# Three buffers in place of two for the weight and activation parts on their way to DRAM, three in place of four for the raw weights on their way in, and theta's raw weights staged in the tiles of z

## The chip, the cores and the metric

The kernel runs on one core of one Trainium2 chip. The metric is device time in microseconds: the median over several runs of one launch, here 564.57 us over 3 runs (564.46 to 564.57). A profile is taken of one further execution of the same program; all durations below come from that execution.

## The reference

What is computed is an attention block followed by two mlp blocks, on 4 batches of 576 tokens with 512 channels (8 heads of 64):

```
scores = q k^T / 8, kept in a window of 32 (heads 0-3) or a window of 128 with every 4th key (heads 4-7)
x  = softmax(scores) v                        # attention, 4 batches
theta = x @ w_theta                           # first mlp ("moe")
zr, zi = x*cos(theta), x*sin(theta)
u  = x + w_tok_r zr + w_tok_i zi              # mixes tokens
x  = u + relu(u @ w_ch)
h  = relu(x @ w_in); u, v = halves of h       # second mlp ("moe2")
v  = layer_norm(v); v = w_spatial v + b_spatial
out = (u*v) @ w_out
```

Several weights (w_theta, w_tok_r, w_tok_i, w_ch, w_in, w_out) reach the kernel as 64-bit floats, and w_spatial as 32-bit floats.

## The kernel before, in words

Every large product is computed from parts: a number is split into a high part and the rest ("hi" and "lo", written as fp32r), and three matmuls (hi*hi, lo*hi, hi*lo) are summed in PSUM. So each weight and each activation passes through a short job before it is used. For a weight the job has these steps: a DMA brings a chunk of raw weights into a staging tile; for 64-bit weights `bits64` builds the 32-bit number with one scaling on ScalarE or GpSimd (L128 or L130) and three operations on VectorE (L131 to L133); one engine copies it into the high part (`copy`, L107 to L111) and one subtracts to get the low part (L144).

Three groups of staging tiles matter here, all rotating (a tile is written again when its last reader is done):

- `w64`: the raw 64-bit chunks, 128 x 576 words of 4 bytes, 2304 bytes in each partition. Four of them. They serve w_theta, w_tok, w_ch, w_in and w_out in turn. The last reader is the first of the three VectorE operations (L131), or the scaling, whichever is later.
- `stage`: the 32-bit number that `bits64` makes, and also the raw w_spatial chunks. Four of them.
- `parts`: a high and a low part side by side, 128 x 2 x 288 numbers, also 2304 bytes in each partition. Two of them. The second mlp's weights don't fit beside the first mlp, so they are split early and their parts are stored to DRAM (`stored`, L152 to L157), 32 times in all: 16 for w_in, 8 for w_spatial, 8 for w_out. The results of the first mlp for batches 0 to 2 go the same way (`ch_run`, L448 to L451), 24 times. A `parts` tile is free again when its store has landed.

The order of the program: attention of batch 0; theta and z of batch 0 (`th_unit`), while the first half of w_tok is prepared; then for each batch the token mixing (`tm_run`) with the attention of the next batch in between, the theta of the next batch, and the channel product (`ch_run`). Batches 2 and 3 are handled together: token mixing of batch 2 goes along with the attention of batch 3, and the 64 tokens left over of both share one theta unit (`th_shared`) that starts from a copy named `xs` (L332). After that follow token mixing and channel product of batch 3 and the second mlp, of dense matmuls. Which jobs of the second mlp's weights stand between which matmuls is set by rates in `spread` (L514, L520, L521).

Each engine runs its instructions in the order of the program. That order is fixed when the kernel is built: a scheduler places the instructions on each engine by its own estimate of durations, with the limits that the rotating tiles set. SyncE issues all DMAs, also in a fixed order, and an issue that must wait holds up those behind it. So a change in the number of buffers moves instructions on every engine, though no line of arithmetic is changed.

z is kept in `zh0` to `zh7` and `zl0` to `zl7`, 128 x 512 numbers each (`ztile`, L321); the first of them is written when the first theta unit with 128 tokens is through.

```
st = const.tile([P, 2 * CH], U32, tag="w64", name="w64", bufs=4)             # L120
t = const.tile([P, 2, CH], F32R, tag="parts", name="parts", bufs=2)[:, :, :n] # L155
pool, n_ = (const, 2) if b < B - 1 else (p2s, 8)                              # L448
h = pz.tile([P, DM], F32R, tag=f"zh{k}", name=f"zh{k}", bufs=bufs)            # L322
```

Of the kernel before, what the change touches and what calls it, by code (L numbers as in the profile page):

```python
# [11 lines left out]
F32 = mybir.dt.float32  # L12
F32R = mybir.dt.float32r
BF16 = mybir.dt.bfloat16
U32 = mybir.dt.uint32
# [6 lines left out]
B, H, S, D = 4, 8, 576, 64  # L22
DM = H * D
P = 128
HALF = S - 4 * P
CH = S // 2
# [5 lines left out]
NA = 6  # L32
NB = NT - NA
NEG = -4.0e9
MAGIC = 1.5 * 2.0**23
TURN = float(np.nextafter(np.float32(2 * math.pi), np.float32(0)))
INV2PI = float(np.float32(1.0 / (2.0 * math.pi)))
# [17 lines left out]
THETA_ENG = "gg"  # L55
# [7 lines left out]
def tile_block(ctx: ExitStack, tc: tile.TileContext, qT, kT, vw, eye_in, mask_in, eye_b_in, w_theta, w_tok, w_ch, w_in, w_sp, w_sph, b_sp, w_out, out):  # L63
# [3 lines left out]
    def f32(ap):  # L67
        return ap.bitcast(F32)


    const = ctx.enter_context(tc.tile_pool(name="const", bufs=1, side="left"))
# [1 line left out]
    dram = ctx.enter_context(tc.tile_pool(name="dram", bufs=1, space=DRAM))  # L73

    ident = const.tile([P, P], F32, name="ident")
    half_pi = const.tile([P, 1], F32, name="half_pi")
    magic = const.tile([P, 1], F32, name="magic")
    masks = const.tile([P, 4, 3, KW], BF16, name="masks")
    eye_b = const.tile([P, P], BF16, name="eye_b")
    V.memset(half_pi, math.pi / 2)  # L80
    V.memset(magic, MAGIC)

# [8 lines left out]
    pz = tc.alloc_tile_pool(name="pz", bufs=1, side="left")  # L91
# [4 lines left out]
    wth_h = pth.tile([P, 4, DM], F32R, name="wth_h")  # L96
    wth_l = pth.tile([P, 4, DM], F32R, name="wth_l")
# [14 lines left out]

    last_dma = [None]

    def bits64(src, n, eng):

        p = src.shape[0]
        st = const.tile([P, 2 * CH], U32, tag="w64", name="w64", bufs=4)  # L120
        last_dma[0] = SY.dma_start(st[:p, :2 * n], src.bitcast(U32))
        w = st[:p, :2 * n].rearrange("p (n w) -> p n w", w=2)
        lw, hw = w[:, :, 0], w[:, :, 1]
        g = const.tile([P, CH], F32, tag="stage", name="w64g", bufs=4)[:p, :n]
        c = c64[:p, :n].bitcast(U32)
        gi = g.bitcast(U32)
        if eng == "a":
            A.mul(g, hw.bitcast(F32), 2.0**-112)  # L128
        else:
            G.tensor_scalar(g, hw.bitcast(F32), 2.0**-56, 2.0**-56, op0=ALU.mult, op1=ALU.mult)  # L130
        V.tensor_scalar(c, lw, 29, None, op0=ALU.logical_shift_right)  # L131
        V.scalar_tensor_tensor(c, gi, 3, c, op0=ALU.logical_shift_left, op1=ALU.bitwise_or)
        V.scalar_tensor_tensor(gi, gi, 0x80000000, c, op0=ALU.bitwise_and, op1=ALU.bitwise_or)  # L133
        return g

    def split_weight(src, hi, lo, eng_hi, eng_lo, eng_bits="g"):
        n = hi.shape[-1]
        if src.dtype == F32:
            s = const.tile([P, CH], F32, tag="stage", name="stage", bufs=4)[:src.shape[0], :n]
            SY.dma_start(s, src)  # L140
        else:
            s = bits64(src, n, eng_bits)
        copy(hi, s, eng_hi)
        (G if eng_lo == "g" else V).tensor_tensor(lo, s, f32(hi), op=ALU.subtract)  # L144

# [6 lines left out]
    def stored(src, dst, k, cs, engs):  # L152

        n = cs.stop - cs.start
        t = const.tile([P, 2, CH], F32R, tag="parts", name="parts", bufs=2)[:, :, :n]  # L155
        split_weight(src[:, k, cs], t[:, 0], t[:, 1], *engs)
        SY.dma_start(f32(dst[:, k, :, cs]), f32(t))  # L157

    def w_theta_job(k, c):
        cs = slice(DM // 2 * c, DM // 2 * (c + 1))  # L160
        split_weight(w_theta[:, k, cs], wth_h[:, k, cs], wth_l[:, k, cs], *THETA_ENG)

    def w_tok_job(k, c):
        cs = slice(CH * c, CH * (c + 1))
# [268 lines left out]
    def ch_run(b):  # L433

        uh, ul = uu.pop(b)
        wch_h, wch_l = wch
        for c in range(2):
            cs = slice(CH * c, CH * (c + 1))
            for e in range(4):
                ps = ps_mm.tile([P, 512], F32, tag="mm", name="ps_r")  # L440
                n = 0
                for k in range(4):
                    for lh, rh in ((wch_h, uh), (wch_l, uh), (wch_h, ul)):
                        PE.matmul(ps[:, :CH], lh[:, k, P * e:P * (e + 1)], rh[:, k, cs], start=(n == 0), stop=(n == 11))  # L444
                        n += 1
                xv = x[b][:, e, cs]
                V.scalar_tensor_tensor(xv, ps[:, :CH], 0.0, xv, op0=ALU.max, op1=ALU.add)
                pool, n_ = (const, 2) if b < B - 1 else (p2s, 8)  # L448
                t = pool.tile([P, 2, CH], F32R, tag="parts", name="parts", bufs=n_)
                split(t[:, 0], t[:, 1], xv, "a", "g")  # L450
                SY.dma_start(f32(x2d[b][:, e, :, cs]), f32(t))  # L451
                yield
# [89 lines left out]
    for hf in (1, 0):  # L542
        cs = slice(DM * hf, DM * (hf + 1))
# [3 lines left out]
    n = 0  # L547
# [6 lines left out]
    p2s = tc.alloc_tile_pool(name="p2s", bufs=1, side="right", reuse_waits="tile")  # L554
# [34 lines left out]
    for _ in ch_run(3):  # L589
        w3()  # L590
# [171 lines left out]
def _layouts(q, k, v, moe_w_theta, moe_w_tok_r, moe_w_tok_i, moe_w_ch, moe2_w_in, moe2_w_spatial, moe2_b_spatial, moe2_w_out):  # L762
# [20 lines left out]
    mask = np.zeros((2, T, 4, 3, KW), np.float32)  # L783
    mask.transpose(0, 2, 3, 1, 4)[:, :, :, (j <= i) | (j > i + WIN)] = NEG
    for n, where in enumerate(starts):
        for h, blk, o in where:
            mask[h, :, n, blk][(i >= o) & (j < o + WIN)] = NEG
    mask = mask.reshape(P, 4, 3, KW)
# [29 lines left out]
```

## Time and profile before

| | |
|---|---|
| median of 3 runs | 564.57 us |
| the profiled execution: its own time | 564.04 us |
| its span, first to last instruction | 562.2 us |
| TensorE busy | 535.4 us (95%) |
| VectorE busy | 323.7 us (58%) |
| GpSimd busy | 261.7 us (47%) |
| ScalarE busy | 245.6 us (44%) |
| DMA moved | 76.07 MB, 135 GB/s over the span |

How to read it: TensorE is close to full over the span as a whole, so a microsecond saved on another engine counts only where TensorE waits for it. The views that say where that is are the busy time in stretches (with the clock that TensorE was granted) and the list of who waited for whom. Line numbers such as L107 are lines of the kernel before; in the changed kernel the same code stands one or two lines later (L107 is L108, L128 is L130, L255 is L257).

### The profile page before, as it was taken

What the parts mean: (1) busy time and instruction counts of PE and PEld (TensorE: products, weight loads), DVE (VectorE), ACT (ScalarE), POOL (GpSimd) and SP (SyncE); (2) the same over time, 40 slices, a digit from 0 to 9 for tenths busy, and PEclk for the clock granted to TensorE, in tenths of its full rate; (3) what the DMA queues carried; (4) which work ended last, traced back from release to release, by engine and by line L of the source; (5) the groups of instructions that cost most, each with busy time, mean ns of one, the idle gap of its engine ahead of it and who ended that gap; (6) DMA issues with size and microseconds to landing.
All of it is one profiled execution on the core that took longest, in us unless ns stands there. A gap on an engine that the chain in (4) does not pass through costs nothing.

```text
span 562.2 us, 11265 instructions
## 1 busy us (share of the span) xinstructions
PE 535.4 (95%) x4148; PEld 477.2 (85%) x4148; DVE 323.7 (58%) x834; ACT 245.6 (44%) x718; POOL 261.7 (47%) x333
## 2 busy tenths in 40 slices
PE   4987999999999999996999999999999999999997
PEld 2765878888888988885979999899899889988996
DVE  2588998898887378656697116763701237353030
ACT  3768855525656444776354112432331224223222
POOL 3483995545975259744269334344201204322040
PEclk9899999999999999998899999999999999999999
DMA  7944956561468352785301999614015110002002
GB/s 188 234 139 126 238 152 194 178 188 62 144 200 236 109 180 96 239 244 170 116 1 43 325 362 355 208 35 136 11 64 168 39 56 1 1 1 76 1 0 94
DMA packets 50079, 76.07 MB, mean 135 GB/s; under 512 B 4068, under 2 KB 30824, under 8 KB 50024
## 3 DMA queue, kind: packets, MB, share of 16 engines
q1 hardware_dynamic: 50024, 75.35, 44.0%
q8 instruction: 33, 0.54, 0.4%
q14 instruction: 22, 0.18, 0.1%
HBM read 52.53 MB, written 22.81 MB: 134 GB/s over the span
## 4 chain that ended last, share of the span: by engine, by line
PE 63%; DVE 11%; DMA 8%; POOL 6%; ACT 5%; issue 5%; SPq 1%; POOLq 0%; DVEq 0%; ACTq 0%
PE ps_y L425 12%; PE ps_sp L693 9%; PE ps_hu L674 9%; PE ps_o L722 9%; PE ps_hv L629 9%; PE ps_r L444 5%; PE s L240 3%; DMA wsp_d<-parts 2%; PE pt L268 2%; DMA win_d<-parts 2%; POOL zl L319 2%; PE ps_x L282 2%; POOL parts L144 1%; DMA qz<-qT 1%; DMA x2d<-parts 1%
## 5 line engine op out<-in xcount | busy, mean ns | idle before, releaser
L425 PE MATMUL ps_y<-wtok_h,zh 128*128 128x288 f32 x270 | 82.7, 309 | 2.4 <-DVE sm L251 1.4
L425 PE MATMUL ps_y<-wtok_h,zl 128*128 128x288 f32 x270 | 81.3, 302 | 0.4 <-POOL zl L319 0.4
L425 PE MATMUL ps_y<-wtok_l,zh 128*128 128x288 f32 x270 | 80.3, 300 | 0.0
L319 POOL TENSOR_TENSOR gl<-hu,gh 128x288 fp32r<-128x288 f32 x32 | 26.0, 814 | 74.5 <-ACT gh L107 74.5
L425 PEld LDWEIGHTS ps_y<-wtok_h,zh 128*128 128x128 f32 x270 | 51.0, 190 | 5.9 <-DVE sm L251 2.1
L697 DVE TENSOR_TENSOR hu<-ps_sp,hu 128x288 f32<-128x288 f32 x32 | 14.6, 456 | 66.7 <-PE ps_sp L696 66.7
L425 PEld LDWEIGHTS ps_y<-wtok_h,zl 128*128 128x128 f32 x270 | 51.3, 190 | 1.9 <-POOL zl L319 0.8
L425 PEld LDWEIGHTS ps_y<-wtok_l,zh 128*128 128x128 f32 x270 | 51.0, 190 | 0.5
L319 POOL TENSOR_TENSOR vl<-hv,vh 128x512 fp32r<-128x512 f32 x16 | 20.9, 1308 | 62.6 <-ACT vh L107 55.2
L258 POOL TENSOR_TENSOR sm<-sm,l 128x288 f32<-128x288 f32 x48 | 32.6, 680 | 27.4 <-DVE l L257 22.1
L255 ACT ACTIVATE sm<-sm,m 128x96 f32<-128x96 f32 x108 | 39.2, 364 | 9.8 <-DVE m L252 7.5
L240 PE MATMUL s<-kt,qz 128*64 128x96 f32 x504 | 35.5, 268 | 4.6 <-DMA qz<-qT 3.4
L319 POOL TENSOR_TENSOR parts<-x,parts 128x288 fp32r<-128x288 f32 x32 | 26.6, 840 | 27.2 <-ACT parts L107 27.2
L693 PE MATMUL ps_sp<-wsp_h,vh 128*128 128x288 f32 x128 | 37.8, 295 | 0.0
L693 PE MATMUL ps_sp<-wsp_l,vh 128*128 128x288 f32 x128 | 37.8, 295 | 0.0
L693 PE MATMUL ps_sp<-wsp_h,vl 128*128 128x288 f32 x128 | 37.8, 295 | 0.0
L674 PE MATMUL ps_hu<-x2h,win_h 128*128 128x288 f32 x128 | 37.7, 294 | 0.0
L674 PE MATMUL ps_hu<-x2h,win_l 128*128 128x288 f32 x128 | 37.7, 294 | 0.0
L674 PE MATMUL ps_hu<-x2l,win_h 128*128 128x288 f32 x128 | 37.7, 294 | 0.0
L444 PE MATMUL ps_r<-uh,wch_l 128*128 128x288 f32 x128 | 37.7, 297 | 0.0
L444 PE MATMUL ps_r<-uh,wch_h 128*128 128x288 f32 x128 | 37.6, 298 | 0.0
L444 PE MATMUL ps_r<-ul,wch_h 128*128 128x288 f32 x128 | 37.4, 296 | 0.0
(180 smaller groups left out, 1570.0 us busy)
## 6 DMA issues: line engine op xcount, KB each, us to landing
x2d<-parts SPq DMA_DIRECT2D x32, 288.0 KB, 2.6
vt<-vw SPq DMA_DIRECT2D x16, 432.0 KB, 4.1
w<-w_tok SPq DMA_DIRECT2D x18, 288.0 KB, 3.0
x2h<-x2d SPq DMA_DIRECT2D x8, 576.0 KB, 7.4
x2l<-x2d SPq DMA_DIRECT2D x8, 576.0 KB, 10.7
kt<-kT SPq DMA_DIRECT2D x15, 304.0 KB, 5.3
w<-w_in SPq DMA_DIRECT2D x16, 256.0 KB, 3.5
win_d<-parts SPq DMA_DIRECT2D x16, 256.0 KB, 2.3
```

The costliest lines, as they stand in the source:

```text
L240: PE.matmul(o, qz[:, j, T * t:T * (t + 1)], kt[:, T * t:T * t + KW], start=not on_pe, stop=not on_pe)
L255: ia = A.activation(sm[:, t, :], src[:, t, :], AF.Exp, bias=m_[:, t:t + 1], scale=scale, accum_out=l[:, t:t + 1])
L258: ig = G.tensor_tensor(sm, sm, l.unsqueeze(2).to_broadcast([P, 3, KW]), op=ALU.mult)
L268: PE.transpose(pt[:KW, P * t:P * (t + 1)], sm[:, t, :], ident)
L319: return (G if el == "g" else V).tensor_tensor(dst_l, src, f32(dst_h), op=ALU.subtract)
L425: PE.matmul(ps[:, :CH], lh[b, k][:, P * d:P * (d + 1)], rh[:, k, cs], start=(n == 0), stop=(n == 3 * len(ks) - 1))
L444: PE.matmul(ps[:, :CH], lh[:, k, P * e:P * (e + 1)], rh[:, k, cs], start=(n == 0), stop=(n == 11))
L629: PE.matmul(ps, lh[:, k, ts_], rh[:, k, DM:], start=(n == 0), stop=(n == 11))
L674: PE.matmul(ps[:, :CH], lh[:, k, fs], rh[:, k, cs], start=(n == 0), stop=(n == 11))
L693: PE.matmul(ps[:, :CH], lh[b, k][:, fs], rh[:, k, cs], start=(n == 0), stop=False)
L697: V.tensor_tensor(t[:, f, cs], ps[:, :CH], t[:, f, cs], op=ALU.mult)
L722: PE.matmul(ps, lh[:, k, ts_], rh[:, k, cs], start=(n == 0), stop=(n == 11))
```

## The change

The `parts` tiles go from two to three, in both places that allocate them. The `w64` tiles go from four to three: both kinds are 2304 bytes in a partition, so the space is the same. Theta's eight raw chunks no longer go through `w64`: each is staged in its own tile out of `zh0` to `zh3` and `zl0` to `zl3`. Two one-column constants become columns of one tile.

```
+PARTS_BUFS = 3
-    half_pi = const.tile([P, 1], F32, name="half_pi")
-    magic = const.tile([P, 1], F32, name="magic")
+    consts = const.tile([P, 2], F32, name="consts")
+    half_pi, magic = consts[:, :1], consts[:, 1:]
...
-    def bits64(src, n, eng):
+    def bits64(src, n, eng, st=None):
-        st = const.tile([P, 2 * CH], U32, tag="w64", name="w64", bufs=4)
+        if st is None:
+            st = const.tile([P, 2 * CH], U32, tag="w64", name="w64", bufs=3)
...
-    def split_weight(src, hi, lo, eng_hi, eng_lo, eng_bits="g"):
+    def split_weight(src, hi, lo, eng_hi, eng_lo, eng_bits="g", st=None):
...
-            s = bits64(src, n, eng_bits)
+            s = bits64(src, n, eng_bits, st)
...
-        t = const.tile([P, 2, CH], F32R, tag="parts", name="parts", bufs=2)[:, :, :n]
+        t = const.tile([P, 2, CH], F32R, tag="parts", name="parts", bufs=PARTS_BUFS)[:, :, :n]
...
-        split_weight(w_theta[:, k, cs], wth_h[:, k, cs], wth_l[:, k, cs], *THETA_ENG)
+        split_weight(w_theta[:, k, cs], wth_h[:, k, cs], wth_l[:, k, cs], *THETA_ENG, st=pz.tile([P, DM], U32, tag=f"z{'hl'[c]}{k}", name="wth64"))
...
-                pool, n_ = (const, 2) if b < B - 1 else (p2s, 8)
+                pool, n_ = (const, PARTS_BUFS) if b < B - 1 else (p2s, 8)
```

The order of instructions moves on every engine. Three places on ScalarE (ACT) follow, each first as before and then as changed.

The first place is the start of batch 3's attention. `sm` is the exponential of the scores (three instructions for one group of scores), `pT` the transposed weights, `x` the attention's result, and `parts<-stage` the high part of a w_spatial chunk. Before:

```order
L255 ACTIVATE sm,l<-sm,m 128x96 x15
L270 COPY pT<-pt 96x384
L255 ACTIVATE sm,l<-sm,m 128x96 x3
L270 COPY pT<-pt 96x384
L107 CAST parts<-stage 128x288
L289 COPY x_3153<-ps_x 128x384
L270 COPY pT<-pt 96x384
L289 COPY x_3153<-ps_x 128x192
L107 CAST parts<-stage 128x288
```

Changed:

```order
L257 ACTIVATE sm,l<-sm,m 128x96 x12
L108 CAST parts<-stage 128x288
L257 ACTIVATE sm,l<-sm,m 128x96 x3
L272 COPY pT<-pt 96x384
L108 CAST parts<-stage 128x288
L257 ACTIVATE sm,l<-sm,m 128x96 x3
L272 COPY pT<-pt 96x384
L108 CAST parts<-stage 128x288
L257 ACTIVATE sm,l<-sm,m 128x96 x3
L108 CAST parts<-stage 128x288
L291 COPY x_3152<-ps_x 128x384
```

The first w_spatial job now stands behind 12 exponentials in place of 18, and four such jobs stand ahead of the first result copy in place of one.

The second place is the end of the same attention. The last four copies to `x` are those of batch 3's last pair of heads, and `parts<-w64g` is the high part of a w_out chunk. Before:

```order
L107 CAST parts<-w64g 128x256
L294 COPY x_3153<-ps_x 128x2x144
L295 COPY x_3153<-ps_x 128x96
L297 COPY x_3153<-ps_x 128x48
L298 COPY x_3153<-ps_x 128x144
L128 ACTIVATE w64g<-w_4123 128x256
L107 CAST parts<-w64g 128x256
L128 ACTIVATE w64g<-w_4134 128x256
L107 CAST parts<-w64g 128x256 x4
```

Changed:

```order
L296 COPY x_3152<-ps_x 128x2x144
L297 COPY x_3152<-ps_x 128x96
L272 COPY pT<-pt 96x384
L108 CAST parts<-w64g 128x256
L299 COPY x_3152<-ps_x 128x48
L300 COPY x_3152<-ps_x 128x144
L272 COPY pT<-pt 96x384 x2
L108 CAST parts<-w64g 128x256
L296 COPY x_3152<-ps_x 128x2x144
L297 COPY x_3152<-ps_x 128x96
L299 COPY x_3152<-ps_x 128x48
L300 COPY x_3152<-ps_x 128x144
```

Before, five w_out jobs stand behind the last copies to `x`; changed, none does: all 8 w_spatial and 8 w_out jobs are ahead of them.

The third place is where the first w_tok chunks meet theta of batch 0 (`w64g<-w` is the scaling of a raw chunk, `ta` and `xh` belong to the theta units). Before:

```order
L128 ACTIVATE w64g<-w_652 128x288
L128 ACTIVATE w64g<-w_661 128x288
L128 ACTIVATE w64g<-w_708 128x288
L128 ACTIVATE w64g<-w_717 128x288
L107 CAST wtok_h<-w64g 128x288
L128 ACTIVATE w64g<-w_763 128x288
L355 ACTIVATE ta<-ps_th,magic 64x512
```

Changed:

```order
L130 ACTIVATE w64g<-w_651 128x288
L130 ACTIVATE w64g<-w_660 128x288
L130 ACTIVATE w64g<-w_707 128x288
L108 CAST wtok_h<-w64g 128x288
L130 ACTIVATE w64g<-w_716 128x288
L357 ACTIVATE ta<-ps_th,consts 64x512
```

The fourth scaling moves behind the first copy, and the fifth behind the theta unit's `ta`.

## Rows read from the trace of the kernel before

**Rows 1.** The page: TensorE's busy time (PE), its weight loads, the other engines.
```profile
PE 535.4 (95%) x4148; PEld 477.2 (85%) x4148; DVE 323.7 (58%) x834; ACT 245.6 (44%) x718; POOL 261.7 (47%) x333
```

**Rows 2.** Stretch, its length; busy PE, PEld, DVE, ACT, POOL; PE's clock, DMA share, GB/s.
```profile
40.00:50.00 10.00, 8.02 (x34) 5.47 (x34) 9.15 (x20) 6.03 (x13) 4.42 (x5) 1.00 0.51 142
150.50:186.60 36.10, 35.64 (x381) 31.45 (x377) 27.10 (x82) 21.55 (x91) 24.54 (x37) 1.00 0.74 216
224.00:272.30 48.30, 41.91 (x447) 36.98 (x446) 30.27 (x88) 30.49 (x117) 26.20 (x36) 0.93 0.68 210
236.40:274.90 38.50, 32.15 (x331) 28.38 (x330) 22.06 (x60) 21.45 (x78) 16.68 (x23) 0.91 0.63 193
262.00:265.30 3.30, 0.50 (x13) 0.39 (x13) 1.40 (x5) 2.39 (x8) 1.08 (x2) 0.82 0.33 114
265.30:270.70 5.40, 5.40 (x23) 5.30 (x24) 5.05 (x10) 1.46 (x5) 2.46 (x3) 0.50 0.54 171
295.60:343.30 47.70, 47.70 (x362) 47.70 (x361) 18.56 (x40) 11.22 (x26) 25.21 (x30) 1.00 0.76 262
320.00:330.00 10.00, 10.00 (x77) 10.00 (x77) 1.05 (x3) 1.97 (x5) 3.85 (x5) 1.00 1.07 372
```

**Rows 3.** Waits of PE, 224 to 272 us: us in total, times, longest.
```profile
PE ps_xn L359 <- DVE xs L332: 2.8, 1, 2.8
...
PE pt L268 <- POOL sm L258: 0.5, 1, 0.5
```

**Rows 4.** Waits of ACT from 236 to 275 us, same columns.
```profile
ACT parts L107 <- DMA wo_d<-parts: 6.4, 3, 3.5
ACT parts L107 <- DMA wsp_d<-parts: 4.3, 4, 2.0
ACT parts L107 <- DMA win_d<-parts: 2.7, 2, 1.4
```

**Rows 5.** ACT in order of time: start us, us, what [idle before <- releaser].
```profile
236.47 0.43 ACT L107 CAST parts<-stage 128x288 fp32r<-128x288 f32 x1 [1.28 <-DMA win_d<-parts]
...
263.65 0.66 ACT L294 COPY x<-ps_x 128x288 f32<-128x288 f32 x1
...
274.43 0.41 ACT L107 CAST parts<-w64g 128x256 fp32r<-128x256 f32 x1 [3.51 <-DMA wo_d<-parts]
```

**Rows 6.** The chain that ended last, 236 to 266 us: start us, us, what.
```profile
248.44 5.90 DMA wsp_d<-parts
...
265.29 0.88 PE ps_xn L359 x3
```

**Rows 7.** SyncE in order of time: the issue of the first w_spatial chunk.
```profile
229.28 0.46 SPq L140 DMA_DIRECT2D stage<-w_sp  x1
```

**Rows 8.** The page on these loads: count, size, median us from issue to landing.
```profile
stage<-w_sp SPq DMA_DIRECT2D x8, 144.0 KB, 2.7
```

**Rows 9.** ACT groups, 236 to 275 us: count, busy us, mean ns, idle before.
```profile
L255 ACT ACTIVATE sm<-sm,m 128x96 f32<-128x96 f32 x18 | 6.5, 362 | 0.0
...
L270 ACT COPY pT<-pt 96x384 f32<-96x384 f32 x6 | 2.9, 482 | 0.0
```

**Rows 10.** ACT at the first w_tok chunks, in order of time.
```profile
43.02 0.46 ACT L128 ACTIVATE w64g<-w 128x288 f32<-128x288 f32 x1 [2.96 <-DMA w<-w_tok]
...
45.17 0.68 ACT L355 ACTIVATE ta<-ps_th,magic 64x512 f32<-64x512 f32 x1
```

**Rows 11.** DVE in the same place and at z's first write, in order of time.
```profile
39.69 0.42 DVE L131 TENSOR_SCALAR c<-w 128x256 uint32<-128x256 uint32 x1
...
41.53 0.46 DVE L131 TENSOR_SCALAR c<-w 128x288 uint32<-128x288 uint32 x1
...
57.01 0.77 DVE L109 CAST zh<-spare 128x512 fp32r<-128x512 f32 x1
```

**Rows 12.** SyncE's waits from 75 to 120 us: us in total, times, longest.
```profile
SPq L121 <- DVE c L131: 22.2, 15, 3.2
```

**Rows 13.** Waits of ACT from 300 to 345 us, same columns.
```profile
ACT parts L107 <- DMA x2d<-parts: 21.9, 6, 5.3
```

## The prediction, made before the changed kernel was run

> **What bounds the kernel now.** I read the page first: TensorE is busy 95% of the span [rows 1], so the question is where the other 5% lies, and whether this change reaches it. The second view is busy time in stretches [rows 2]. From 295.6 us on TensorE is busy without a break (47.70 of 47.70 us there, and the second mlp behind it is more of the same), so what happens on other engines after that point costs nothing; whatever moves the start of that part moves the end by as much. The stretch 224.0 to 272.3 us is different: token mixing of batch 2 with the attention of batch 3, TensorE busy 41.91 of 48.30 us, so 6.39 us idle, where the same kind of work for batch 1 and attention 2 (150.5 to 186.6) has 0.46 us idle. Inside it stands a second loss: from 265.3 to 270.7 us the granted clock is 0.50, the lower of TensorE's two levels (1.2 GHz), right after a stretch in which TensorE was busy 0.50 of 3.30 us. 5.4 us at half speed cost 2.7 us. So up to 6.39 + 2.7 = 9.1 us are to be had here.
>
> The third view is TensorE's waits in this stretch [rows 3]: five of them make up the 6.4 us, the longest 2.8 us for `xs`, the copy of the last tokens of batch 3, and each ends on a copy of the attention, mostly by ScalarE. Why these come late is the fourth view, ScalarE's own waits [rows 4]: 6.4 + 4.3 + 2.7 = 13.4 us for a `parts` tile whose store hadn't landed. ScalarE works in order, so each such wait holds up the attention's copies behind it. The chain of waits shows one such store, 5.90 us on the path, and its end: TensorE's transposes of `xs` at 265.29 [rows 6].
>
> **The change part by part.**
>
> *Third parts tile, last token-mixing stretch (the main term).* The 16 high-part casts of w_spatial and w_out run from 236.47 to 274.43 us [rows 5]: 15 steps in 37.96 us, 2.53 us each. With two tiles, one tile's turn (cast, subtraction, store, landing) takes two steps, 5.06 us. Three tiles with the same turn give a step of 5.06 / 3 = 1.69 us. But the order changes too, and ScalarE gets more to do between the casts. In the changed order, first place, six exponentials more stand behind the first cast (24 in place of 18), and ten `pT` copies instead of six stand ahead of the attention's end. ScalarE is busy 21.45 us in the stretch of the 16 casts [rows 2]; six exponentials at 362 ns and four copies at 482 ns [rows 9] add 2.2 + 1.9 us, so 25.5 us, or 1.70 us per step if it never waits. Two floors of 1.7 us don't overlap perfectly; I take 1.8 us.
>
> The first cast needs its chunk: issued at 229.28 [rows 7], landing 2.7 us later [rows 8], 232.0. In the order before it also stood behind six more exponentials and two copies, and then waited 1.28 us for a tile [rows 5]. I take 233.0; the ends are 231.5 and the old 236.5.
>
> In the changed order, second place, all 16 casts precede the last copies to `x`. So the last cast is at 233.0 + 15 x 1.8 = 260.0, its own step takes 0.3, and from the first of the last copies to TensorE's transposes it is 265.29 - 263.65 = 1.64 us [rows 5, 6]. The transposes start at 261.9, 3.4 us sooner. TensorE itself can be there by then: 265.29 less its four other waits (6.39 - 2.8 = 3.6) and less this one is 258.9.
>
> *The clock.* If TensorE's idle time ahead of the transposes shrinks from 6.39 to about 3 us, the fall to the lower level may not come: between 40 and 50 us TensorE is busy 8.02 of 10 us and its clock stays at 1.00 [rows 2]. But one gap of some 2 us may still bring it. Ends 0 and 2.7 us; no row decides between them, so I take half, 1.35 us.
>
> *Third parts tile elsewhere.* From 300 to 345 us ScalarE waits 21.9 us for stores of batch 2's results [rows 13], the largest sum of all, and TensorE doesn't notice [rows 2]. It is worth nothing now. It would count only if the second mlp's loads came too late; they stand behind these stores on SyncE's queue, and with three tiles the stores come sooner. Value 0.
>
> *One w64 tile less.* SyncE waits 22.2 us in 15 waits for VectorE to read a raw chunk between 75 and 120 us [rows 12], 1.5 us each, so the tiles are already waited for with four. With three, each load is issued one job later, and attention loads queue behind it. The 15 loads take 45 us, 3 us per job, so a load has two jobs, 6 us, in place of three for a landing of about 3 us. Value 0, cover that margin; ends 0 and +1.5 us, one such wait reaching TensorE.
>
> *Theta staged in z.* Theta's eight loads no longer wait, and its last raw chunk is read at 39.69 while z is first written at 57.01 [rows 11]: 17 us apart, so the shared tiles add no wait. The first three w_tok loads also go out at once. The fourth, which now waits 2.96 us on ScalarE until 43.02 [rows 10], does not gain: its tile is that of the first, read until 41.53 + 0.46 [rows 11], so it lands about 3 us later, near 45. In the changed order, third place, that scaling is the last ahead of `ta`, and the fifth, which was ahead of it before, comes later. `ta` starts near 45.2, as now [rows 10]. Value 0, ends -1.8 and +1.8, the shift of the fourth scaling.
>
> *The two constants in one tile.* The same two memsets, long before their readers: 0.
>
> The sum against the profiled execution: 564.04 - 3.4 - 1.35 = 559.29 us. That execution lies 0.53 us under the median, so the median of the changed kernel should be 559.8 us.
>
> **The rivals.** *A, all of it is given back:* the casts go at 1.7 us from 232.0, the transposes start at 232.0 + 25.5 + 1.94 = 259.4 (5.9 us sooner), and the clock stays up, 2.7 us: 564.57 - 8.6 = 556.0. For it: the idle of the like stretch for batch 1. Against: ScalarE would have to be busy all the time, and it waits for TensorE and VectorE too.
>
> *B, slower: the stores set the pace, not the tiles.* If three stores in flight take longer to land than two, a tile's turn grows and the step stays near 2.5 us, while now 16 casts, not 11, stand ahead of the last copies. The break-even step is (265.29 - 1.94 - 233.0) / 15 = 2.02 us, a turn of 6.1 us. At a step of 2.3 us the transposes start at 233.0 + 34.5 + 1.94 = 269.4, 4.1 us later, the clock falls as now, and the time is 568.7. For it: one store took 5.90 us [rows 6], and ScalarE is now tied to five more of them. Against: in this stretch the DMA engines are busy 0.63 of the time at 193 GB/s, while they reach 1.07 and 372 GB/s at 320 to 330 us [rows 2], so there is room for a third store. The Trainium skill ("Trainium Kernel Development and Optimization", section Key Constraints) says that DMAs of all queues run on the same 16 DMA engines and interleave. If that sharing were the limit here, the step would remain 2.53 us and the transposes would come at 272.9, 572.2 us in all; the share of 0.63 speaks against the full form.
>
> *C, no change:* the step is near 2.0 us, or the w64 queue loses early what the parts win, or TensorE's idle time only moves to other copies: 564.5. For it: the new order was planned on estimates, and so was the old one, which ended in five waits. Against: the 13.4 us that ScalarE loses to tiles are real.
>
> **How the numbers follow.** My forecast, a gain of 2 to 7 us, 0.46; A 0.17; C 0.15; B 0.22. Differences of this kernel under 0.2% (1.1 us) can't be told from no change. So faster 0.63, same 0.15, slower 0.22. The range goes from 556.0, case A, to 567.5, some way into B; below it I leave about 6 in 100, above it 14. My forecast's own range is 557.5 to 562.5.
>
> **What would show it.** Right: ScalarE's waits for `parts` between 230 and 262 us well under 13.4 us; 16 casts about 1.8 us apart; transposes of `xs` near 262; TensorE's idle time in this stretch near 3 us and its clock at 1.00 behind it, or 0.50 for a shorter time; from there on everything earlier by the same amount. Wrong: a step of 2.0 us or more with landings over 6 us (B); waits that move to the raw chunks of w_spatial or w_out, because SyncE is held up; `ta` of the first theta unit later than 45.2, or TensorE waiting for `wtok` between 60 and 112 us (the w64 term).

## The result, and the profile after

The changed kernel takes 571.01 us (median of 6 runs, 568.73 to 572.82); the kernel before, measured beside it, 564.50 us. The ratio is 1.0118, 95% interval 1.0092 to 1.0144: 1.2% slower, where 0.8% faster was forecast. The profiled execution of the changed kernel took 569.66 us, with a span of 567.8 us.

The page first. It answers to [rows 1]: TensorE's work is the same, so the 5.6 us by which the span grew (562.2 to 567.8) are idle time and a lower clock (0.987 to 0.982 over the span).

```profile
PE 535.9 (94%) x4148; PEld 479.9 (85%) x4148; DVE 328.2 (58%) x830; ACT 244.9 (43%) x722; POOL 261.5 (46%) x333
```

Where they are is told by TensorE's progress in the two traces, in us from the start of the span:

| the instruction | before | changed | difference |
|---|---|---|---|
| token mixing of batch 1 begins (217th ps_y matmul) | 142.38 | 141.82 | -0.6 |
| channel product behind it (97th ps_r) | 192.64 | 195.24 | +2.6 |
| token mixing of batch 2 begins (433rd ps_y) | 218.24 | 221.71 | +3.5 |
| transposes of `xs` | 265.29 | 273.65 | +8.4 |
| first theta unit of batch 3 (181st ps_th) | 278.41 | 284.15 | +5.7 |
| first matmul of the second mlp (ps_hv) | 343.18 | 349.02 | +5.8 |

So the loss is made in the token mixing of batches 1 and 2 (3.2 us in the first, 4.9 us from the start of the second to the transposes). The first of these had not been in the prediction at all. The next fence is the changed kernel's busy time in stretches (columns as in [rows 2]), in three of them TensorE's idle time and the clock behind it.

```profile
150.50:160.00 9.50, 7.64 (x48) 6.97 (x47) 8.73 (x23) 3.17 (x18) 9.27 (x14) 0.82 0.65 197
153.16:158.00 4.84, 4.84 (x26) 4.68 (x27) 4.51 (x13) 2.26 (x12) 4.84 (x8) 0.65 0.61 205
224.00:279.50 55.50, 46.56 (x487) 41.38 (x484) 31.72 (x94) 32.18 (x122) 30.20 (x39) 0.91 0.67 205
228.97:235.20 6.23, 6.23 (x34) 5.95 (x36) 4.49 (x12) 3.33 (x18) 6.00 (x7) 0.50 0.86 263
264.73:269.12 4.39, 0.00 (x0) 0.03 (x1) 2.82 (x7) 2.53 (x7) 1.87 (x3) 1.00 0.38 133
269.12:273.65 4.53, 3.49 (x42) 2.88 (x43) 0.71 (x3) 3.21 (x11) 1.47 (x3) 0.62 0.74 232
301.28:349.02 47.74, 47.74 (x360) 47.74 (x361) 18.79 (x39) 10.60 (x26) 23.93 (x28) 1.00 0.78 268
```

The stretch 224.0 to 279.5 us answers to the one of [rows 2] from 224.0 to 272.3: TensorE idle for 55.50 - 46.56 = 8.9 us, where it was 6.4. From 150.5 to 160.0 the clock is 0.82 on average: there are 1.86 us without a matmul, and in the 4.84 us behind them the clock is 0.65. From 228.97 it is 0.50 for 6.23 us, again right behind a gap, and from 269.12 it is 0.62, behind the longest gap. The last row, as before, is full: what is late at 301 us stays late to the end.

TensorE's waits from 224 to 279.5 us (us in total, times, longest) answer to [rows 3]. The wait for `xs` shrank from 2.8 to 1.0 us; a wait of 4.4 us ahead of the transposes `pt` and one of 1.9 us for a masked score `sm` are new. The first has no releaser in the row ("issue"). It lies between the attention's products, which end at 264.73, and 269.12, right behind the copies to `x` that begin at 268.18. It is gone in e6 below, where these copies come sooner; that they free the PSUM tile that `pt` needs is read from this order, and no row says it.

```profile
PE pt L270 <- issue: 4.4, 1, 4.4
PE ps_y L427 <- DVE sm L253: 1.9, 1, 1.9
...
PE ps_xn L361 <- DVE xs L334: 1.0, 1, 1.0
```

In the token mixing of batch 1 (142 to 224 us) there is one more of the second kind, of 1.9 us too.

What VectorE did in these two places is in its order of time (start, us, what, and in brackets the idle time before it and who ended it). First batch 1: three casts of w_in parts (line 110, two in one row) stand between the second score and the third, which TensorE waits for. In the kernel before one such cast of 0.28 us stood there.

```profile
146.67 0.44 DVE L253 SCALAR_TENSOR_TENSOR sm<-s,masks 128x288 f32<-128x288 f32 x1
147.03 1.64 DVE L110 CAST parts<-w64g 128x256 fp32r<-128x256 f32 x2
...
151.20 1.25 DVE L110 CAST parts<-w64g 128x256 fp32r<-128x256 f32 x1
...
152.66 0.44 DVE L253 SCALAR_TENSOR_TENSOR sm<-s,masks 128x288 f32<-128x288 f32 x1
```

Then the start of batch 3's attention. The cast waits 2.45 us for a `parts` tile, one whose store of batch 1's results had to land, and the scores stand behind it:

```profile
226.85 0.50 DVE L110 CAST parts<-w64g 128x256 fp32r<-128x256 f32 x1 [2.45 <-DMA x2d<-parts]
...
228.47 0.44 DVE L253 SCALAR_TENSOR_TENSOR sm<-s,masks 128x288 f32<-128x288 f32 x1
```

The kernel before at the same place: the same wait, 1.44 us, but three scores ahead of it, and TensorE goes on.

```profile
222.46 0.45 DVE L251 SCALAR_TENSOR_TENSOR sm<-s,masks 128x288 f32<-128x288 f32 x1
...
223.28 0.45 DVE L251 SCALAR_TENSOR_TENSOR sm<-s,masks 128x288 f32<-128x288 f32 x1
...
224.00 0.44 DVE L251 SCALAR_TENSOR_TENSOR sm<-s,masks 128x288 f32<-128x288 f32 x1
...
226.60 1.43 DVE L109 CAST parts<-w64g 128x256 fp32r<-128x256 f32 x1 [1.44 <-DMA x2d<-parts]
```

This is what the change did: with a third tile the scheduler, which plans on its own estimates, placed these casts earlier on an engine that works in order. (In e1 below, with two tiles, no wait for a score is longer than 0.5 us.) In batch 1 the casts simply take VectorE's time ahead of the score; in the second place the tile was not free yet either.

ScalarE answers to [rows 4, 5] with the casts of w_spatial and w_out (the first, the first of the late copies to `x`, and the last cast):

```profile
237.47 0.42 ACT L108 CAST parts<-stage 128x288 fp32r<-128x288 f32 x1
...
268.18 0.67 ACT L296 COPY x<-ps_x 128x288 f32<-128x288 f32 x1
...
270.84 0.40 ACT L108 CAST parts<-w64g 128x256 fp32r<-128x256 f32 x1
```

The 16 casts go from 237.47 to 270.84 us, 33.37 / 15 = 2.22 us each. ScalarE's waits in that time:

```profile
ACT parts L108 <- DMA wsp_d<-parts: 2.8, 2, 2.5
ACT w64g L130 <- DMA w<-w_out: 2.7, 3, 1.6
ACT parts L108 <- DMA stage<-w_sp: 1.6, 1, 1.6
...
ACT parts L108 <- DMA win_d<-parts: 0.8, 1, 0.8
ACT parts L108 <- DMA wo_d<-parts: 0.5, 2, 0.3
```

For `parts` it now waits 2.8 + 0.8 + 0.5 = 4.1 us, where it was 13.4 [rows 4]. So the third tile took away waits for a tile, as was expected of it. But 2.7 us are new waits for raw w_out chunks and 1.6 us for a raw w_spatial chunk.

### The profile page after: what moved, and what is told of

Its sections match the earlier page's. It is cut to its first block, busy times and chain, and to the rows that moved or that the text cites. A ratio compares the mean times of both kernels' runs of the same rounds, so it can differ in the third digit from the quotient of the medians.

```text
span 567.8 us, 11280 instructions
## 1 busy us (share of the span) xinstructions
PE 535.9 (94%) x4148; PEld 479.9 (85%) x4148; DVE 328.2 (58%) x830; ACT 244.9 (43%) x722; POOL 261.5 (46%) x333
## 4 chain that ended last, share of the span: by engine, by line
PE 65%; DVE 11%; DMA 9%; ACT 5%; issue 5%; POOL 3%; SPq 2%; ACTq 0%; POOLq 0%; DVEq 0%
PE ps_y L427 13%; PE ps_hu L676 9%; PE ps_sp L695 9%; PE ps_o L724 9%; PE ps_hv L631 9%; PE ps_r L446 6%; PE ps_th L349 3%; PE s L242 2%; ACT sm L257 2%; DMA wth<-w_theta 1%; DMA wsp_d<-parts 1%; DMA kt<-kT 1%; PE ps_x L284 1%; DVE tb L365 1%; PE pt L270 1%
## 5 line engine op out<-in xcount | busy, mean ns | idle before, releaser
L427 PE MATMUL ps_y<-wtok_l,zh 128*128 128x288 f32 x270 | 81.5, 303 | 0.0
L427 PEld LDWEIGHTS ps_y<-wtok_h,zh 128*128 128x128 f32 x270 | 52.2, 194 | 8.3 <-DVE sm L253 5.1
L427 PEld LDWEIGHTS ps_y<-wtok_l,zh 128*128 128x128 f32 x270 | 52.2, 194 | 0.2
L321 POOL TENSOR_TENSOR ul<-x,uh 128x288 fp32r<-128x288 f32 x32 | 26.2, 829 | 32.5 <-ACT uh L108 32.4
```

The source lines that it names most:

```text
L321: return (G if el == "g" else V).tensor_tensor(dst_l, src, f32(dst_h), op=ALU.subtract)
L427: PE.matmul(ps[:, :CH], lh[b, k][:, P * d:P * (d + 1)], rh[:, k, cs], start=(n == 0), stop=(n == 3 * len(ks) - 1))
```

## The experiments

Theory 1: the order costs the time, 1a on VectorE (casts of w_in ahead of the scores), 1b on ScalarE (casts and scalings ahead of the last copies to `x`). Theory 2: the missing raw tile (raw tiles are the `w64` tiles). Theory 3: theta staged in z. Theory 5 (no theory has the number 4): the third parts tile by itself, in any order. All kernels were timed in 5 rounds against the kernel before. Ratios are to that kernel, with 95% intervals.

**The numbers of tiles.** From the changed kernel:

```
e1  -PARTS_BUFS = 3
    +PARTS_BUFS = 2
e2  -tag="w64", name="w64", bufs=3)       +... bufs=4)
    -masks = const.tile(...)              +masks = pth.tile(...)
e3  PARTS_BUFS = 2 and w64 bufs=4
```

e1. 

> The change with two parts tiles in place of three (raw w64 tiles three, theta staged in z, all as in the changed kernel). Its VectorE and ScalarE have the casts of the second mlp's weights in the same places among the attention's instructions as the kernel before. Theory 1 (the third tile lets the scheduler put these casts ahead of the attention's work on engines that work in order, and that order costs the time): 564.5 us, 563 to 566, no idle time of TensorE ahead of an sm of VectorE at 150 to 155 us or 227 to 229 us, transposes of xs within 2 us of 265.3. Theory 2 (three raw tiles make the loads of raw chunks late, and the engines wait for those): 569 to 572 us, ScalarE waits for raw w_out chunks ahead of the last copies to x. Theory 3 (theta staged in z upsets the start): 567 us or more, with the loss in place before 60 us.

e2. 

> The change with four raw w64 tiles again beside the three parts tiles; room for it is made by placing the masks, used by the attention alone, in a pool that is released before the second mlp. Theory 1: still slow, 567 to 572 us, because the casts stand ahead of the attention as in the changed kernel: two idle stretches of TensorE near 151 and 227 us of some 2 us each, with the clock at 0.50 behind them. Theory 2: 560 to 564 us, the waits for raw chunks are gone and with them the 4.4 us ahead of the last transposes. Theory 3: as the changed kernel, 571 us.

e3. 

> Of the change only theta's raw chunks staged in z and the two constants in one tile; two parts tiles and four raw tiles as before. Theories 1 and 2: 564.5 us, within 1.5 us. Theory 3: 567 us or more, with ta of the first theta unit later than 45.2 us and TensorE late from there to the end.

Measured: e1 565.27 us, 1.0030 [1.0010, 1.0050]; e2 568.36 us, 1.0086 [1.0054, 1.0118]; e3 563.37 us, 1.0006 [0.9979, 1.0033], with single runs from 561.13 to 569.23 us. So theta's staging costs nothing that can be measured, and theory 3 falls. The third parts tile costs 0.80% with four raw tiles (e3 to e2) and 0.88% with three (e1 to the changed kernel), some 4.7 us; the missing raw tile costs 0.24% and 0.32%, 1.4 to 1.8 us, which the intervals of one such pair don't clear; more pairs follow. The third tile costs most. Whether through the order or by itself these three can't tell. In e2 ScalarE waits for no raw w_out chunk any more, but 6.4 us for `parts` tiles, and the transposes of `xs` still come at 272.89: the missing raw tile is not what makes them late.

**Ties.** `behind` queues the instructions that a job puts on ScalarE, VectorE and GpSimd behind given instructions of the same engine. Here it ties each job of the second mlp's weights behind the softmax that was last put into the program:

```
+    def pinned(f):
+        m = max(softmax)
+        behind(softmax[m], f) if m >= 12 else f()
...
-    second = jobs(j_in + j_sp + j_out)
+    second = jobs([lambda f=f: pinned(f) for f in j_in + j_sp + j_out])
```

e4 ties all jobs, e5 the first twelve of `j_in`, e6 `j_sp` and `j_out`; e7 is e4 with PARTS_BUFS = 2.

e4. 

> The changed kernel with its three parts tiles, and each job of the second mlp's weights tied, on ScalarE, VectorE and GpSimd, behind the softmax that was last put into the program when the job was (from batch 1 on). So the casts can no longer be moved ahead of that softmax, and 13 of the 16 casts of w_spatial and w_out stand behind batch 3's last copies to x. Theory 1: the idle stretches near 151, 227 and 264 us go (1.9 + 1.9 + 4.4 us) and the lower clock behind them, some 3 us: 571 - 11 = 560 us, 557 to 564. Theory 2: only the last of the three goes, 566 to 568 us. Theory 3: 571 less some of that, but the 2.8 us of the start stay, 563 us or more.

Measured: 566.53 us, 1.0061 [1.0039, 1.0083]. The three idle stretches of TensorE (near 151, 227 and 265 us) went, and the transposes of `xs` come at 263.52, 1.8 us sooner than before the change. But then TensorE waits for `zh` of a theta unit, because 13 casts now stand behind the last copies to `x`, among the theta units of batch 3. TensorE in order of time, and the clock behind that wait:

```profile
263.52 0.63 PE L361 MATMUL ps_xn<-ident,xs 128*128 128x128 f32 x4 [1.35 <-DVE xs L334]
...
280.99 0.61 PE L427 MATMUL ps_y<-wtok_h,zh 128*128 128x288 f32 x1 [4.06 <-ACT zh L108]
```

```profile
280.00:290.00 10.00, 9.02 (x34) 7.48 (x35) 9.08 (x19) 5.35 (x11) 5.35 (x7) 0.71 0.29 93
```

The time lies where theory 2 had it (566 to 568 us), but by another way: that theory had only the last of the three stretches go. Theory 1 holds in the middle, and its sum (560 us) missed what the moved casts would do at their new place.

e5. 

> The changed kernel; only the first twelve w_in jobs, those put among the attention of batch 2, are tied behind the softmax last put into the program. ScalarE's casts of w_spatial and w_out stay ahead of batch 3's last copies to x. Theory 1a (casts on VectorE ahead of the softmax cost the time): the idle stretch at 151 us and its lower clock go, 2.8 us by TensorE's progress between 142 and 193 us: 568 us, 567 to 569.5. Theory 1b (casts and scalings on ScalarE ahead of the last copies to x cost it): 571 us, 570 to 572. Theory 5 (the third tile costs by itself, through its stores, in any order): 571 us.

Measured: 565.10 us, 1.0028 [1.0007, 1.0049]; that is 0.90% or 5.1 us less than the changed kernel, more than theory 1a expected (2.8 us), since the second gap shrank as well. On VectorE no cast stands among the first three scores of batch 1's stretch, and the clock stays up in both places:

```profile
149.42 0.81 DVE L253 SCALAR_TENSOR_TENSOR sm<-s,masks 128x288 f32<-128x288 f32 x2
...
154.99 0.44 DVE L253 SCALAR_TENSOR_TENSOR sm<-s,masks 128x288 f32<-128x288 f32 x1
```

```profile
150.50:160.00 9.50, 8.91 (x78) 7.99 (x76) 7.50 (x21) 6.56 (x27) 6.99 (x9) 1.00 0.42 125
222.00:236.00 14.00, 12.68 (x133) 11.16 (x132) 13.02 (x32) 8.81 (x33) 13.41 (x16) 1.00 0.62 185
```

The wait for a `pt` tile remains, 3.0 us of it, and the time is nearly that of the kernel before all the same: theory 1a carries most of the loss. Two things are read from the traces alone. The tie moves whole jobs, with VectorE's and GpSimd's work on the raw chunks, and no run moves the casts by themselves. And the cast at the second place is the thirteenth, which isn't tied: it still stands ahead of the score, but waits 0.94 us for its tile in place of 2.45.

```profile
PE pt L270 <- ACT x L291: 3.0, 1, 3.0
PE ps_y L427 <- DVE sm L253: 1.6, 2, 1.0
```

e6. 

> The changed kernel; only the jobs of w_spatial and w_out are tied behind the softmax last put into the program; the w_in casts on VectorE stand as in the changed kernel. On ScalarE six casts stand ahead of the last copies to x and ten behind them. Theory 1a: 570 us or more, the stretches at 151 and 227 us stay. Theory 1b: the 4.4 us ahead of the last transposes go, transposes of xs before 269 us; but the ten casts now stand among the theta units of batch 3, where thirteen of them took some 7 us back in the kernel with all jobs tied, so 566 to 569 us. Theory 5: 571 us.

Measured: 567.02 us, 1.0078 [1.0049, 1.0106]. The 4.4 us for `pt` are gone and the transposes of `xs` come at 266.91, but the ten moved casts cost a wait for `zh`, as in e4:

```profile
PE ps_y L427 <- ACT zh L108: 3.4, 1, 3.4
```

So 1b is worth some 2 us, and only if the casts find a place that costs less.

e7. 

> The kernel with all jobs tied behind the softmax last put into the program, with two parts tiles in place of three (raw tiles three, theta staged in z). VectorE and ScalarE have nearly the order of the three-tile kernel with all jobs tied, so the number of tiles is all that differs there. Theory 1: in a like order the third tile costs nothing and may help: the two-tile kernel takes as long as the three-tile one or longer, 566 to 570 us. Theory 5: the two-tile kernel is faster by 3 us or more, 563.5 us or less.

Measured: 564.02 us, 1.0012 [0.9994, 1.0029], 0.49% under e4. Neither theory hit: theory 1 expected no gain from two tiles, theory 5 more. The orders of e4 and e7 differ on every engine, against what had been expected, so this pair doesn't hold the order fixed.

**The last ten jobs later.** e8 to e12 tie all jobs and put the last ten into the token mixing of batch 3, behind its last z. e9 to e12 also load x2 of batch 0 (the first mlp's result, which the second mlp reads) ahead of half of win (the parts of w_in). Their sources differ in the numbers of tiles alone (and e11 has the masks placed as in e2); the order that the scheduler makes of them differs too.

```
-    spread(th_run(PAIR + 1, ...), (chain(...), TAIL_RATE), (second, 2.5))
+    spread(th_run(PAIR + 1, ...), (chain(...), TAIL_RATE))
     for _ in tm_run(3, K_ALL):
         n += 1
+        next(second, None)
+        next(second, None)
```

e8. 

> The changed kernel with all jobs tied behind the softmax last put into the program, and the last ten of them (two of w_spatial, eight of w_out) put into the token mixing of batch 3, tied behind its last z. So they stand neither ahead of the last copies to x nor among the theta units of batch 3. Theory 1: the loss of the kernel with all jobs tied was in the theta units of batch 3 (7.2 us between 278 and 301 us by TensorE's progress against the kernel before); without it 559.5 us, 558 to 563. If the stores that are now later hold up the loads of the second mlp, TensorE waits for win or wsp after 310 us and it is 565 us or more. Theory 5: 566 us as with all jobs tied.

e9. 

> The kernel with all jobs tied and the last ten put into the token mixing of batch 3, and besides x2 of batch 0 loaded ahead of the first half of win, not behind all of win (TensorE waited 2.5 us at its first hv matmul in the kernel without this). Three parts tiles, three raw tiles. It is one of four that differ in the two numbers of tiles alone. Theory 1 (in a tied order the third parts tile costs nothing; the raw tile that is missing costs 1.4 us at the start): 560 us, the wait at the first hv is gone. Theory 5 (the third parts tile costs 2.8 us also in a tied order, the difference between the two pinned kernels): 560 us here, and 557 in the kernel with two parts tiles and three raw ones.

e10. 

> As the last kernel with two parts tiles and four raw ones, the numbers of the kernel before (theta staged in z). Theory 1: 558.6 us. Theory 5: 555.8 us.

e11. 

> As the last two with three parts tiles and four raw ones (the masks in a pool released before the second mlp, for room). Theory 1: 558.6 us, the same as with two parts tiles. Theory 5: 558.6 us, 2.8 us over the one with two parts tiles.

e12. 

> As the last three with two parts tiles and three raw ones. Theory 1: 560 us, the same as with three parts tiles and three raw ones. Theory 5: 557 us, 2.8 us under it.

Measured: e8 562.58 us, 0.9986 [0.9967, 1.0005]; e9 564.04, 0.9997 [0.9981, 1.0014]; e10 575.90, 1.0215 [1.0190, 1.0241]; e11 561.73, 0.9968 [0.9947, 0.9989]; e12 577.59, 1.0249 [1.0223, 1.0275]. Both theories are far off for two tiles, which lose 2.5% to three, and 3 to 4 us too fast for three. In e8 TensorE is 3.9 us ahead of the kernel before from 309 us on, and gives 2.5 us back in front of its first hv matmul. The load of x2 was not the cause, since the wait is the same in e9, where that load comes sooner. VectorE's last operation on a raw chunk (line 135) and TensorE's first hv matmul, e8:

```profile
347.84 0.42 DVE L135 SCALAR_TENSOR_TENSOR w64g<-w64g,c 128x256 uint32<-128x256 uint32 x1
348.36 0.47 PE L637 MATMUL ps_hv<-win_h,x2h 128*128 128x512 f32 x1 [2.55 <-issue]
```

And e10, with two tiles, where that last chunk comes 10 us later:

```profile
357.92 0.42 DVE L135 SCALAR_TENSOR_TENSOR w64g<-w64g,c 128x256 uint32<-128x256 uint32 x1
358.44 0.77 PE L638 MATMUL ps_hv<-win_h,x2h 128*128 128x512 f32 x1 [16.19 <-issue]
```

In both, and in e9, e11 and e12, the matmul starts 0.52 us after the start of that operation. `c64`, the scratch tile of `bits64`, is a PSUM bank that is given to the second mlp's first tile.

**The bank of c64 kept apart.** e13 is e11 and e14 is e10 with this edit; e15 and e16 are without it and tie the first twelve w_in jobs only, with four raw tiles and three or two parts tiles.

```
+    ps_t = tc.alloc_tile_pool(name="ps_t", bufs=3, space=PSUM)   # now behind ps_v
-    ps_v.release()                                               # now at the end
-    ps_2 = tc.alloc_tile_pool(name="ps_2", bufs=4, space=PSUM)
+    ps_2 = tc.alloc_tile_pool(name="ps_2", bufs=3, space=PSUM)
```

e13. 

> Three parts tiles, four raw ones, all jobs tied and the last ten in the token mixing of batch 3, and c64's PSUM bank kept to the end, so that the second mlp's tiles take three banks in place of four and its first hv matmul need not wait for the last raw weight. If that wait (2.5 us) was c64's bank: no wait ahead of the first hv, 561.7 - 2.5 = 559.2 us, 558 to 560.5. If it was the loads of win or x2: the wait stays and it is 561.7 us or, with one bank less, more.

e14. 

> The same with two parts tiles. If its 16.2 us ahead of the first hv matmul were c64's bank alone: 575.9 - 16.2 = 559.7 us, as with three tiles, and the third tile is worth nothing in a tied order. If the third tile is worth something for the jobs that come late: 562 us or more, and TensorE waits for wsp or wo in the second mlp. If it costs by itself: 557 us or less.

e15. 

> The change with four raw tiles (masks in a pool released early), and the first twelve w_in jobs tied behind the softmax last put into the program. By e5 (1.0028) less the missing raw tile (0.3%): 1.000, 562.5 to 565 us. If the prediction's main term, earlier casts in the attention of batch 3, is worth anything, it shows here as a ratio under 0.998.

e16. 

> The same with two parts tiles, so the kernel before but for theta's staging and the ties of the first twelve w_in jobs. If the third tile has no worth in a held order: as e15 within 0.2%. If it costs 2.8 us as in the two kernels with all jobs tied: a ratio 0.5% below e15's.

Measured: e13 559.91 us, 0.9927 [0.9905, 0.9948]; e14 559.31 us, 0.9912 [0.9886, 0.9937]; e15 563.34 us, 0.9997 [0.9982, 1.0013]; e16 568.81 us, 1.0077 [1.0057, 1.0097]. In e13 the first hv matmul no longer waits for that operation:

```profile
346.08 0.42 DVE L135 SCALAR_TENSOR_TENSOR w64g<-w64g,c 128x256 uint32<-128x256 uint32 x1
343.89 0.39 PE L637 MATMUL ps_hv<-win_h,x2h 128*128 128x512 f32 x1
```

The bank was the wait, and e13 and e14 beat both kernels: 0.7 to 0.9% under the kernel before. From 224.0 to 279.5 us TensorE now idles 55.50 - 53.84 = 1.7 us, at full clock:

```profile
224.00:279.50 55.50, 53.84 (x534) 47.05 (x531) 37.10 (x94) 31.15 (x109) 25.66 (x34) 1.00 0.47 141
```

e15 closes the account of the change: e5 and the raw tile's 0.3% had forecast 1.000. So the jobs of w_in on VectorE and the missing raw tile make up the whole loss, and the earlier casts of w_spatial and w_out on ScalarE, which were the prediction's main term and stand in e15 too, bring no gain that can be measured (it was to show as a ratio under 0.998; the transposes of `xs` come at 268.96 there). e16 was expected at e15 or below and is 0.80% above it: with two tiles the jobs' operations stand between those of the theta units of batch 2 on VectorE, and TensorE waits for `ta` there.

```profile
PE ps_r L446 <- DVE ta L358: 3.4, 1, 3.4
```

The third parts tile over all orders:

| order | two tiles | three tiles | the third tile's worth |
|---|---|---|---|
| the scheduler's, four raw tiles | 1.0006 (e3) | 1.0086 (e2) | +0.80% |
| the scheduler's, three raw | 1.0030 (e1) | 1.0118 (the change) | +0.88% |
| first twelve tied, four raw | 1.0077 (e16) | 0.9997 (e15) | -0.80% |
| all tied, three raw | 1.0012 (e7) | 1.0061 (e4) | +0.49% |
| all tied, last ten later, four raw | 1.0215 (e10) | 0.9968 (e11) | -2.47% |
| the same, three raw | 1.0249 (e12) | 0.9997 (e9) | -2.52% |
| the same, c64's bank kept, four raw | 0.9912 (e14) | 0.9927 (e13) | +0.15% |

No line holds the order fixed: the number of tiles changes it each time. The worth's sign goes with the order, so theory 5 falls. Where TensorE waits for few of these jobs (the last line) the intervals of the two kernels overlap.

## Why the prediction was wrong, point by point

**The step that failed first** is "third parts tile elsewhere ... Value 0". It looked for the tile's other users in the stores of batch 2's results alone, where nothing waits. That was right of those stores, but it left out the w_in jobs among the attention of batch 2 and ahead of batch 3's, whose casts VectorE makes. The changed order moved them ahead of the scores; the prediction compared the order of ScalarE in three places and that of VectorE in none. The term is +5.1 us (e5 against the changed kernel), not 0. None of the rivals had it: B was the slower one, through the pace of the stores. Its premise came true, since w_spatial's stores landed after 4.4 us in place of 2.9, and its numbers came near: a step of 2.3 us where 2.22 was measured, transposes 4.1 us later where 8.4 - 3.5 = 4.9 us were lost in that stretch. But the waits for tiles did not stay; they fell to 4.1 us, and e5 got back the time with these casts in place. So B's nearness is in part luck. The changed kernel's DMA issues from 236 to 274 us (count, size, median us to landing):

```profile
wsp_d<-parts SPq DMA_DIRECT2D x8, 288.0 KB, 4.4
wo_d<-parts SPq DMA_DIRECT2D x8, 256.0 KB, 2.6
```

**The main term** (-3.4 us) failed at the step "the step of 1.8 us". That ScalarE's waits for `parts` would shrink was right (13.4 to 4.1 us), the gain from it was not. The waits that went were replaced by others. ScalarE from the first cast to the first of the last copies in the kernel before, and from the first cast to the last in the changed one:

```profile
236.47:263.65 27.18, 22.46 (x285) 19.23 (x283) 16.04 (x48) 17.70 (x68) 12.69 (x18) 1.00 0.70 213
237.47:270.84 33.37, 27.77 (x324) 24.67 (x326) 20.16 (x63) 23.33 (x91) 18.21 (x26) 0.98 0.80 246
```

The prediction had 27.0 us for the second row, 25.5 of work and 1.5 idle. The work is 23.3 us, somewhat less; the idle time is 10.0 us: 4.1 for tiles, 4.3 for raw chunks, 1.4 for TensorE's `pt`. In the kernel before it was 27.18 - 17.70 = 9.5 us, and of the 13.4 us for tiles only 7.0 stood ahead of these copies (4.3 + 2.7 [rows 4]). The other 6.4, for w_out's stores, stood behind them and couldn't hold them up (the last ended at 274.43 [rows 5], 10.8 us behind the first copy). So ScalarE had less to gain than 13.4 us, and five more jobs to do ahead of the copies. The step was 2.22 us, over the break-even of 2.02: the "same turn" did not hold, since landings grew, and waits for raw chunks came in place of those for tiles. The last cast was at 270.84, not 260.0. The first came at 237.47, not 233.0: its chunk was issued at 230.40, near the 229.28 of [rows 7], but the cast stood behind exponentials that VectorE's late scores held up. The transposes of `xs` came 8.4 us later, not 3.4 us sooner, of which 3.5 us had come in from the stretches before. That raw chunks would be waited for if SyncE was held up stood among the signs of "wrong". In e4, with the casts behind, they came 1.8 us sooner: about half of what was forecast was to be had, by another order.

Its reading of [rows 3] was loose as well: of the five waits two end on ScalarE (1.3 and 1.0 us), two on VectorE (2.8 and 0.8) and one on GpSimd (0.5), so not most of them on ScalarE. The longest does stand behind ScalarE's copies [rows 6].

**The clock.** It was taken at half of 2.7 us, regained behind `xs`. Behind `xs` it was at 1.00 (273.65 to 275.23 us), but only since the lower level had come sooner, with the gap of 4.4 us: 0.62 from 269.12 to 273.65 us, up to 4.53 x 0.38 = 1.7 us. And the two gaps of 1.9 us on VectorE's scores brought the lower level in places where it had not been: 4.84 x 0.35 = 1.7 us and 6.23 x 0.50 = 3.1 us. That "one gap of some 2 us may still bring it" was right, for gaps that the prediction did not see.

**One raw tile less.** Taken at 0, with +1.5 as the end; it costs 1.4 to 1.9 us in five pairs of kernels (e3 to e1, e2 to the changed kernel, e11 to e9, e10 to e12, e15 to e5). It seems to be lost early: at the first channel product (111.56 us before) nine profiled executions with three raw tiles are 2.2 us late on average, eight with four 0.6 us; single ones scatter from -1.0 to +3.9. So the margin of 6 us for a landing of 3 did not cover it, or the loss is elsewhere; which wait ends last there was not pursued, and the cause stays open.

**Theta in z** was right: 1.0006 for e3. The fourth scaling waited for its chunk and `ta` came at 43.83, a little ahead of the 45.2 expected:

```profile
43.46 0.46 ACT L130 ACTIVATE w64g<-w 128x288 f32<-128x288 f32 x1 [1.30 <-DMA w<-w_tok]
43.83 0.67 ACT L357 ACTIVATE ta<-ps_th,consts 64x512 f32<-64x512 f32 x1
```

**Everything from 301 us on as late as at 301** was right.

**The chances.** 0.22 stood for slower, all of it on B; the mechanism that came had none.

Left open: why e7 is 0.49% faster than e4; and the 0.9 us that the changed kernel loses between 193 and 222 us.

## What to carry to other kernels

Where a scheduler fixes the order, one buffer more is a change of order on every engine. Compare that order on each engine that the bottleneck waits for, at each place where a moved instruction can wait for a transfer, and not only where the buffer was short. The Trainium skill ("Perfetto Trace Analysis", section Optimization Strategy) takes regular gaps as a sign that room for the next tile may be missing; here the waits for the tile shrank to a third and the time rose, since on VectorE casts moved ahead of scores that TensorE waits for. Tie background jobs behind the work that the bottleneck waits for first, and choose the number of buffers then, by measuring: in the best order found (e13, e14) two and three were alike, in other tied orders they lay 0.5 to 2.5% apart, either way round.

## What the runs showed of the hardware

A gap of 1.9 us without a matmul brought the clock to its lower level twice (0.65 on average over 4.84 us, 0.50 over 6.23 us); in e5, where the second gap was 1.0 us, it stayed at 1.00 from 222 to 236 us. But the length of a gap alone doesn't decide it. The gap of 2.55 us ahead of the first hv matmul left the clock up in e8 and brought it down in e9 (and in e11). The 5 us behind it, e8 and then e9:

```profile
348.36:353.36 5.00, 5.00 (x22) 4.14 (x23) 1.93 (x7) 1.93 (x3) 0.14 (x1) 1.00 1.04 381
348.67:353.67 5.00, 5.00 (x15) 3.97 (x16) 0.89 (x4) 0.39 (x1) 0.13 (x1) 0.66 1.03 357
```

VectorE's cast of a 128x256 tile took 0.28 to 1.40 us in one execution. The long one below stood beside a GpSimd operation (230.94 to 232.23 us), the short one in a time when GpSimd was idle. VectorE and then GpSimd of the changed kernel, each in order of time:

```profile
230.98 1.40 DVE L110 CAST parts<-w64g 128x256 fp32r<-128x256 f32 x1
...
236.63 0.28 DVE L110 CAST parts<-w64g 128x256 fp32r<-128x256 f32 x1
230.94 1.29 POOL L321 TENSOR_TENSOR zl<-ta,zh 128x512 fp32r<-128x512 f32 x1
...
237.00 0.73 POOL L146 TENSOR_TENSOR parts<-w64g,parts 128x256 fp32r<-128x256 f32 x1 [1.75 <-DVE parts L110]
```

The Trainium skill ("GPSIMD Engine Reference", section Key points) says that GpSimd shares its SBUF interfaces with VectorE, and that some of VectorE's instructions contend with it there; these rows agree in that. The page names instructions in a two-port mode or with two SBUF inputs; the cast has one input, and no run shows in which mode it runs. So a job's cast that moves ahead of a score can cost several times its shortest time where GpSimd is busy.
